# A gated scan and a mixture of experts on one core: one padded transpose per block, wider evictions, more row buffers

## The chip, the core and the metric

The kernel runs on one core of a Trainium2 chip. A core has five engines with queues of their own: PE (TensorE, matmuls), DVE (VectorE), ACT (ScalarE), POOL (GpSimd) and SP (SyncE, which here only issues transfers). Each takes its instructions strictly in the order of the program. The metric is device time of one execution, in microseconds; smaller is better.

## The reference

Two stages follow each other. The first is a gated linear recurrence over 5056 steps, for 4 sequences of 256 features; the second sends each of the 20,224 resulting rows to one of 8 experts, chosen by the largest of its 8 gate logits.

```python
a_t = exp(8 * sigmoid(r_gate) * log(clip(sigmoid(a_param), 1e-6, 1 - 1e-6)))
x_gated = sqrt(max(1 - a_t * a_t, 1e-6)) * sigmoid(i_gate) * x
for t in range(S):
    h = a_t[:, t] * h + x_gated[:, t]
    y[:, t] = h
...
e_idx = argmax(x @ w_gate, axis=1)               # x is now y, one row for each token
for e in range(8):
    rows = e_idx == e
    h = maximum(x[rows] @ w1[e], 0)              # 256 -> 1024
    out[rows] = gate_w[rows] * sigmoid(x[rows] @ w_output_gate)[e] * (h @ w2[e])
```

## The kernel before

**Work and order.** Each operation is described as a piece of `Work` with an engine, a cost, what it waits for and a rank; a planner (`in_order`) plays the list through and fixes the order of PE, DVE and ACT. The constants at the top of the file (ranks, costs, lags) set that order. SP and POOL issue in the order in which the pieces come out of it.

**Scan.** Tokens lie in 21 chunks: two of four tiles of 128 tokens, then of eight, the last of six. A block is up to four tiles, 512 tokens, with features on partitions (two halves of 128). For each block SP loads `rt`, `it` and `xt` (r_gate, i_gate, x; line 597, 512 KB each), from rings of 4, 3 and 2 buffers. ACT computes the gates (`gate_r` L603, `gate_i` L606, the decay L613, the square L617, the root L622), DVE the gated input (L609, L625) and the scan (L656).

**Routing.** From the third chunk on, DVE finds the peak of a chunk (L742), from it comes a scale (L760 to L764), and the states are split in two planes of 16 bit, a high part by ACT (`high`, L771) and a rest by DVE (`rest_of`, L774), written over the block's `rt` tile. PE takes the gate logits from the planes (L791), and DVE adds their three parts (L800 to L802), chooses the expert and counts positions. Beside this, SP turns the planes from features on partitions to tokens on partitions with DMA transposes (`flip`, L781), into row buffers `rows_all`, eight tiles deep. DVE writes a weight and a token number behind each row (`weights`, L891 and L892), and POOL scatters the rows by expert into a table `xs` in DRAM (L401), one indirect transfer for each tile.

**Experts.** A slot is 128 or 256 consecutive rows of one expert in `xs`. There are 104 slots at fixed places, worked off while the scan goes on, then 29 that are planned at run time (and a loop for more, which these inputs don't need). For a slot SP fetches the rows with a DMA transpose (`xt<-xs`, L1036). PE computes the hidden layer in eight blocks `f` of 128 (L1091, six matmuls each, into PSUM tiles `ph`, a ring of three); ACT evicts with a ReLU to the high part of `h` (L1106), DVE to the rest (L1109); PE multiplies with the second weights (L1148, into `po`); ACT scales (L1160, `ot`, two buffers) and POOL stores the 128 rows by an indirect transfer (L1163). One eviction covers two blocks `f`, so 256 columns for a slot of 128 rows and 512 for one of 256. The weights of the experts are loaded by ACT's queue and split in two planes in the first part of the run.

## Time and profile before

| | |
|---|---|
| time, median of 3 runs | 1096.76 us (1094.14 to 1097.5) |
| the profiled execution's own time | 1096.72 us |
| its span, first to last instruction | 1094.9 us |
| mean granted TensorE clock | 0.947 of full speed |
| PE, DVE, ACT, POOL busy | 954.1, 722.6, 639.2, 366.0 us |
| indirect transfers of POOL (L401, L1163) | 158 and 165 |
| DMA transposes on SP (L781, L1036) | 152 and 133 |

Busy is the time in which an engine ran something; matmuls are pipelined, so a busy PE need not be at its peak. A row of the profile names line, engine, operation and tiles as output<-input. SPq and POOLq are the queues of these engines, where transfers are issued and waits are held. In brackets behind a row stands the idle time of the engine just before it, and what ended it.

### The profile page before, as it was taken

To read this page: it belongs to the slowest core of one execution; us is meant where nothing else is said; L and a number is where in the kernel's file an instruction comes from. 1 tells how busy PE (TensorE), PEld (TensorE's weight loads), DVE (VectorE), ACT (ScalarE), POOL (GpSimd) and SP (SyncE) were. 2 spreads that over 40 slices of the span, in tenths; PEclk is the share of its full clock that TensorE was granted. 3 is DMA by queue.
4 is the path that set the end of the run, shared out by engine and by line. 5 is a ranking of instruction groups with operands and counts; after the bars stand their busy time and mean duration, and the time that the engine had idled before them with its cause. 6 is when DMAs were issued, how large, how long until landed. Compare 5 with 4: busy or idle time off the path is not lost. (4 is left out here: it accounts for less than half of the span.)

```text
span 1094.9 us, 30254 instructions
## 1 busy us (share of the span) xinstructions
PE 954.1 (87%) x11462; PEld 875.1 (80%) x11462; DVE 722.6 (66%) x1987; ACT 639.2 (58%) x1137; POOL 366.0 (33%) x341
## 2 busy tenths in 40 slices
PE   2628369998899899899999999999999999999993
PEld 1527368888889889888988887888888889999992
DVE  4898998878778769877987687778622222343330
ACT  5995977757757757776786667764222222333331
POOL 1112343353336236344633353435322122121111
PEclk9659679999999999999999999999999999999997
DMA  9969588886877967989887766755612213999970
GB/s 335 391 218 224 160 192 195 152 210 174 204 168 177 200 157 179 191 203 183 187 207 201 187 172 195 200 129 118 199 51 52 54 45 114 246 238 240 242 200 14
DMA packets 263764, 197.22 MB, mean 180 GB/s; under 512 B 203036, under 2 KB 214046, under 8 KB 263616
## 3 DMA queue, kind: packets, MB, share of 16 engines
q1 hardware_dynamic: 237536, 136.23, 53.7%
q0 software_dynamic: 15552, 42.23, 11.8%
q10 hardware_dynamic: 10528, 16.78, 4.4%
q8 instruction: 95, 1.56, 0.6%
q14 instruction: 53, 0.43, 0.2%
HBM read 79.09 MB, written 45.28 MB: 114 GB/s over the span
## 5 line engine op out<-in xcount | busy, mean ns | idle before, releaser
L1148 PE MATMUL po<-w2r,h 128*128 128x256 f16 (+1 forms) x3960 | 523.4, 275 | 1.2 <-ACT ot L1160 0.9
L1091 PE MATMUL ph<-xt,w1r 128*128 128x128 f16 (+1 forms) x4992 | 436.4, 239 | 56.4 <-DVE h L1109 43.0
L1091 PEld LDWEIGHTS <-w1r 128*128 128x128 f16 x4992 | 369.0, 100 | 84.7 <-issue 55.6
L1148 PEld LDWEIGHTS <-h 128*128 128x128 f16 x3960 | 372.6, 99 | 40.5 <-ACT h L1106 0.8
L1109 DVE SCALAR_TENSOR_TENSOR h<-ph,h 128x256 f16<-128x256 f32 (+1 forms) x532 | 236.4, 481 | 222.2 <-ACT h L1106 219.3
L1163 POOL DMA_INDIRECT out_dram<-ot,osc x165 | 185.9, 1127 | 490.1 <-ACT h L1106 264.4
L1106 ACT ACTIVATE h<-ph 128x256 f16<-128x256 f32 (+1 forms) x532 | 209.1, 431 | 185.5 <-PE po L1148 158.0
L401 POOL DMA_INDIRECT xs<-rows_all,posi x158 | 176.6, 1118 | 214.7 <-ACT h L1106 74.4
L1160 ACT ACTIVATE ot<-po,osc 128x256 f32<-128x256 f32 x165 | 74.3, 471 | 120.3 <-PE po L1148 66.2
L1091 PE MATMUL ph<-xt,ws 128*128 128x128 f16 x1392 | 98.4, 219 | 0.0
L656 DVE TENSOR_TENSOR_SCAN it<-rt,last,it 128x512 f32<-128x512 f32 (+4 forms) x78 | 96.0, 1240 | 0.4
L1091 PEld LDWEIGHTS <-ws 128*128 128x128 f16 x1392 | 88.4, 98 | 2.9
L609 DVE SCALAR_TENSOR_TENSOR xt<-it,xt 128x1024 f32<-128x1024 f32 (+1 forms) x40 | 48.2, 1207 | 42.6 <-ACT it L606 35.8
L606 ACT ACTIVATE it<-it 128x1024 f32<-128x1024 f32 (+1 forms) x40 | 41.8, 1044 | 57.7 <-DMA it<-in_i_gate_dram 57.6
L625 DVE SCALAR_TENSOR_TENSOR it<-it,xt 128x1024 f32<-128x1024 f32 (+1 forms) x40 | 48.2, 1205 | 21.9 <-ACT it L622 21.9
L613 ACT ACTIVATE rt<-rt,lam 128x512 f32<-128x512 f32 (+1 forms) x80 | 62.0, 803 | 0.9 <-issue 0.3
L774 DVE SCALAR_TENSOR_TENSOR rt<-it,scale,rt 128x1024 f16<-128x1024 f32 (+1 forms) x38 | 47.6, 1266 | 10.6 <-ACT rt L771 10.2
L617 ACT ACTIVATE it<-rt 128x1024 f32<-128x1024 f32 (+1 forms) x40 | 41.8, 1044 | 18.2 <-DVE xt L609 18.0
L603 ACT ACTIVATE rt<-rt 128x1024 f32<-128x1024 f32 (+1 forms) x40 | 41.9, 1046 | 13.2 <-DMA rt<-in_r_gate_dram 11.7
L742 DVE TENSOR_REDUCE peak<-it 128x1 f32<-128x1024 f32 (+1 forms) x38 | 45.4, 1196 | 0.0
L622 ACT ACTIVATE it<-it,quarter 128x1024 f32<-128x1024 f32 (+1 forms) x40 | 45.2, 1137 | 0.3
L771 ACT ACTIVATE rt<-it,scale 128x1024 f16<-128x1024 f32 (+1 forms) x38 | 42.3, 1133 | 2.2 <-DVE scale L764 2.1
(168 smaller groups left out, 564.8 us busy)
## 6 DMA issues: line engine op xcount, KB each, us to landing
ws<-w1r SPq DMA_DIRECT2D x58, 512.0 KB
rt<-in_r_gate_dram SPq DMA_DIRECT2D x39, 512.0 KB
it<-in_i_gate_dram SPq DMA_DIRECT2D x39, 512.0 KB
xt<-in_x_dram SPq DMA_DIRECT2D x39, 512.0 KB
w1r<-in_moe_w_dram ACTq DMA_DIRECT2D x7, 1024.0 KB
w2r<-in_moe_w_dram ACTq DMA_DIRECT2D x7, 1024.0 KB
out_dram<-ot,osc POOLq DMA_INDIRECT x165
xs<-rows_all,posi POOLq DMA_INDIRECT x158
```

What stands on the lines that cost most here:

```text
L401: op = nc.gpsimd.indirect_dma_start(out=xs[:, :], out_offset=bass.IndirectOffsetOnAxis(ap=pos, axis=0), in_=rows.bitcast(F32), in_offset=None,
L609: nc.vector.scalar_tensor_tensor(t("xt"), t("it"), 1.0, t("xt"), op0=ALU.add, op1=ALU.mult)
L613: nc.scalar.activation(r[:, h], r[:, h], AF.Exp, scale=lam[:, h:h + 1], bias=lam[:, h:h + 1])
L625: nc.vector.scalar_tensor_tensor(t("it"), t("it"), 0.5e-3, t("xt"), op0=ALU.max, op1=ALU.mult)
L656: nc.vector.tensor_tensor_scan(H[:, h, lo:hi], A[:, h, lo:hi], H[:, h, lo:hi], first, op0=ALU.mult, op1=ALU.add)
L774: nc.vector.scalar_tensor_tensor(halves(key, 1, m), tiles["it", key][:, :, 0:m], tiles["scale_of", c], halves(key, 0, m), op0=ALU.mult, op ...
L1091: nc.tensor.matmul(ph[:, i, 0:w], lhsT=ws[:, f // 2 % 2, a, c, i * P:(i + 1) * P], rhs=xt[:, b * ND + c, 0:w], start=k == 0, stop=k == 3 * ...
L1106: newest["relu"] = nc.scalar.activation(part(0, f0), tiles["ph", s, f0][:, :, 0:w], AF.Relu).ins
L1109: nc.vector.scalar_tensor_tensor(part(1, f0), tiles["ph", s, f0][:, :, 0:w], 0.0, part(0, f0), op0=ALU.max, op1=ALU.subtract)
L1148: nc.tensor.matmul(po[0:pw, j], lhsT=hh[:, a, f % 4, j * P:j * P + pw], rhs=second(b), start=f + j + a + b == 0, stop=f == NF - 1 and a == ...
L1160: nc.scalar.activation(ot[0:pw], tiles["po", s][0:pw, j], AF.Copy, scale=tiles["osc", s][0:pw, j, 0:1])
L1163: op = nc.gpsimd.indirect_dma_start(out=out[:, :], out_offset=bass.IndirectOffsetOnAxis(ap=tiles["osc", s][0:pw, j, 1:2].bitcast(I32), axi ...
```

## The change

- **Planes.** The two planes of a block lie tile by tile, 640 elements apart, of which 512 are data. `high` and `rest_of` write them in this form; `rest_of` becomes two instructions and clears the gaps between the tiles. One DMA transpose turns the whole block, 19 groups of 128 columns for four tiles, where before there were four transposes of four. The row buffers have the same pitch of 640, so the transposed padding covers the place of weight and token number, and `weights` waits for the transposes.
- **Logits.** Their three parts are added by one reduction.
- **Evictions.** A PSUM tile holds four blocks `f` of a slot of 128 rows, and one eviction covers them, 512 columns. For slots of 256 rows nothing changes.
- **Buffers.** Twelve row buffers in place of eight, three `xt` buffers in place of two; GpSimd's scratch for transfer descriptors is set to 4096 bytes; a small tile is kept in 16 bit, and one that nothing reads is left out.
- **A drain** of GpSimd's queue stands behind the store of the slot that is eight before the end.
- **Planner.** Costs, lanes of transfers in flight and all ranks are new; the decay is described in four pieces in place of one.

```diff
-XT = 2
-ROWS = 8
+XT = 3
+ROWS = 12
+PITCH = 640
+PLANE = 2 * PITCH - P // 2
-LAG = 0.0015
+LAG = 0.00132
...
+    RETIRE = n_slots - GROUP - 8
...
+        def plane(key, k, h, j):
+            at = j * PITCH + (k * ND + h) * P
+            return tiles["planes", key][:, at:at + P]
...
         def rest_of(key, m):
-            nc.vector.scalar_tensor_tensor(
-                halves(key, 1, m), tiles["it", key][:, :, 0:m], tiles["scale_of", c], halves(key, 0, m), op0=ALU.mult, op1=ALU.subtract
-            )
-
-        def flip(b, key, k, m):
+            if m > P:
+                a = plane(key, 2, 0, 0)
+                nc.vector.memset(bass.AP(a.tensor, a.offset, [a.ap[0], [PITCH, m // P - 1], [1, P]]), 0.0)
+            for h in range(ND):
+                nc.vector.scalar_tensor_tensor(
+                    halves(key, 1, m // P)[:, :, h], of_tiles(key, m)[:, :, h], tiles["scale_of", c], halves(key, 0, m // P)[:, :, h],
+                    op0=ALU.mult, op1=ALU.subtract,
+                )
+
+        def flip(b, key, m):
             nb = m // P
-            for h in range(ND):
-                queue("SP", nc.sync.dma_start_transpose(
-                    rows_all[:, row_at[b]:row_at[b] + nb, (k * ND + h) * P:(k * ND + h + 1) * P], halves(key, k, m)[:, h],
-                ))
+            to = rows_all[:, row_at[b]:row_at[b] + nb, :].rearrange("p j (k d) -> p (j k) d", d=P)
+            runs = nb * PITCH // P - 1
+            queue("SP", nc.sync.dma_start_transpose(to[:, 0:runs], tiles["planes", key][:, 0:runs * P]))
...
-            u = small.tile([P, 4, 2 * E], F32, name=f"lt_{c}_{b}", tag="lt", bufs=1)[:, 0:nb]
-            nc.vector.tensor_copy(u, t[:, :, 2])
-            nc.vector.tensor_tensor(u, u, t[:, :, 1], op=ALU.add)
-            nc.vector.tensor_tensor(st("lz", 2 * E)[:, b:b + nb], u, t[:, :, 0], op=ALU.add)
+            nc.vector.tensor_reduce(st("lz", 2 * E)[:, b:b + nb], t.rearrange("p j k e -> p j e k"), axis=AX.X, op=ALU.add)
...
-        wt = work("DVE", 0.68, weights, [zs], quick, uses=rused)
+        wt = work("DVE", 0.73, weights, [zs] + flips, quick, uses=rused)
...
-        for f0 in range(0, NF, 2):
+        g = 2 * SLOT // w if WIDER else 2
+        for f0 in range(0, NF, g):
             pu, pold = rings["ps_h"].new()
-            for i in range(2):
+            for i in range(g):
...
+                if s == RETIRE:
+                    queue("Pool", nc.gpsimd.drain(fusable=False), "out")
...
-    nc = _bacc.Bacc("TRN2", target_bir_lowering=False, num_devices=1)
+    nc = _bacc.Bacc("TRN2", target_bir_lowering=False, num_devices=1, dynamic_dma_scratch_size=4096)
```

The tables of ranks show little in themselves; what they do is seen in the order of the instructions. The first place is SP's queue at the tenth chunk: the transposes of its first block (`rt_0`) and second (`rt_4`), the i_gate loads (`it_4`, `it_0`) of the blocks after it, and the next slot's fetch (`xt<-xs`). Before:

```order
L781 DMA_TRANSPOSE rows_all<-rt_0_4325 128x4x128 x4
L597 DMA it_4_5859<-in_i_gate_dram 128x2x512
L597 DMA it_0_5874<-in_i_gate_dram 128x2x512
L597 DMA rt_0_5927<-in_r_gate_dram 128x2x512
L1028 TENSOR_LOAD firsti_5250
L1036 ISA
L1036 DMA_TRANSPOSE xt_40_5991<-xs 128x4x128
```

and now:

```order
L626 DMA it_4_5428<-in_i_gate_dram 128x2x512
L626 DMA it_0_5441<-in_i_gate_dram 128x2x512
L823 DMA_TRANSPOSE rows_all<-rt_0_4351 128x19x128
L823 DMA_TRANSPOSE rows_all<-rt_4_4472 128x19x128
L1065 TENSOR_LOAD firsti_3577
L1073 ISA
L1073 DMA_TRANSPOSE xt_39_5557<-xs 128x4x128
```

The loads have moved from behind the first block's four transposes to a place ahead of both blocks' transposes; in other chunks the first load stands ahead of the first block's transpose and the second between the two. The second block's transposes follow at once, where before they stood behind two more fetches.

The second place is DVE's queue in the same chunk, just ahead of `weights` (it ends with the write to `rows_all`). The names are `h` for an eviction, `osc` for a slot's scales, `it` for the scan. Before:

```order
L872 TENSOR_REDUCE sm_6014<-ex_5982 128x8
L873 TENSOR_REDUCE zs_6012<-df_5970 128x8
L609 SCALAR_TENSOR_TENSOR xt_4_5581<-it_4_5859,xt_4_5581 128x1024
L1109 SCALAR_TENSOR_TENSOR h_1_6017<-ph_4_5943,h_1_6017 128x2x128
L1109 SCALAR_TENSOR_TENSOR h_1_6017<-ph_6_5972,h_1_6017 128x2x128
L1121 TENSOR_SCALAR osc_6072<-mt_5628,tab 128x1
L1122 SCALAR_TENSOR_TENSOR osc_6072<-again_3700,mt_5628 128x1
L880 TENSOR_SCALAR zs_6012<-zs_6012 128x8
L881 SCALAR_TENSOR_TENSOR sm_6014<-sm_6014,zs_6012 128x8
L885 TENSOR_SCALAR sm_6014<-sm_6014,scale_5733 128x8
L891 RECIPROCAL rows_all<-sm_6014 128x8
```

and now:

```order
L1147 SCALAR_TENSOR_TENSOR h_0_5735<-ph_0_5661,h_0_5735 128x4x128
L685 SCALAR_TENSOR_TENSOR it_0_4780<-rt_0_4973,last_4_5220,it_0_4780 128x512
L688 COPY last_0_5779<-it_0_4780 128x2
L1147 SCALAR_TENSOR_TENSOR h_1_5776<-ph_4_5713,h_1_5776 128x4x128
L1159 TENSOR_SCALAR osc_5813<-mt_5377,tab 128x1
L1160 SCALAR_TENSOR_TENSOR osc_5813<-again_3580,mt_5377 128x1
L917 TENSOR_SCALAR zs_5604<-zs_5604 128x8
L918 SCALAR_TENSOR_TENSOR sm_5606<-sm_5606,zs_5604 128x8
L922 TENSOR_SCALAR sm_5606<-sm_5606,scale_5302 128x8
L928 RECIPROCAL rows_all<-sm_5606 128x8
```

`weights` has moved behind the counts of the chunk and a scan of the next; between the second block's split and the write to `rows_all` there now stand seven evictions of 512 columns, two scans and three instructions of 1024 columns, and some thirty small ones.

## Rows read from the trace of the kernel before

**Rows 1.** The page: busy time, share of the span, instructions.

```profile
PE 954.1 (87%) x11462; PEld 875.1 (80%) x11462; DVE 722.6 (66%) x1987; ACT 639.2 (58%) x1137; POOL 366.0 (33%) x341
```

**Rows 2.** Busy time by stretch: length, engines, PEclk (granted clock), DMA share, GB/s.

```profile
0.00:219.00 219.00, 133.24 (x1607) 121.56 (x1608) 185.31 (x489) 171.24 (x258) 60.35 (x64) 0.82 0.85 234
219.00:739.00 520.00, 484.54 (x6081) 444.95 (x6080) 411.25 (x1088) 361.33 (x622) 224.81 (x197) 0.98 0.77 185
739.00:1067.00 328.00, 326.87 (x3672) 300.31 (x3671) 123.39 (x403) 103.35 (x249) 77.93 (x78) 1.00 0.56 150
1067.00:1095.00 28.00, 9.45 (x109) 8.31 (x106) 2.64 (x10) 3.32 (x9) 2.95 (x3) 0.71 0.04 14
```

**Rows 3.** Waits from 219 to 739 us: total, times, longest.

```profile
PE ph L1091 <- DVE h L1109: 28.5, 17, 3.7
...
PE pk L862 <- DVE oh L856: 5.9, 3, 2.7
```

**Rows 4.** Timeline of one stall: start, duration, operation, count, idle before.

```profile
349.94 5.53 SPq L781 DMA_TRANSPOSE rows_all<-rt  x4
349.94 1.28 DVE L774 SCALAR_TENSOR_TENSOR rt<-it,scale,rt 128x1024 f16<-128x1024 f32 x1 [0.37 <-ACT rt L771]
...
355.52 1.12 SPq L597 DMA_DIRECT2D it<-in_i_gate_dram  x2
...
362.09 1.06 ACT L606 ACTIVATE it<-it 128x1024 f32<-128x1024 f32 x1 [3.69 <-DMA it<-in_i_gate_dram]
...
363.05 0.64 ACT L1106 ACTIVATE h<-ph 128x256 f16<-128x256 f32 x2
...
364.79 1.51 PE L1091 MATMUL ph<-xt,w1r 128*128 128x128 f16 x17 [3.65 <-DVE h L1109]
```

**Rows 5.** Waits from 219 to 739 us, of ACT and DVE for transfers.

```profile
ACT it L606 <- DMA it<-in_i_gate_dram: 49.3, 22, 5.1
...
DVE rows_all L891 <- DMA xs<-rows_all,posi: 3.1, 2, 2.7
```

**Rows 6.** The end: timeline of PE and POOL; drains (min/median/max ns).

```profile
1071.50 4.95 PE L1148 MATMUL po<-w2r,h 128*128 x42
...
1077.29 0.98 POOL L1163 DMA_INDIRECT out_dram<-ot,osc  x1 [1.88 <-ACTq L1243]
...
L1271 POOLq DRAIN  x3: 40/103/9216, 1084.9 to 1094.7; - x3
```

**Rows 7.** Transposes of SP (L781 all, L1036 from 780 to 905), min/median/max ns.

```profile
L781 SPq DMA_TRANSPOSE rows_all<-rt x152: 1167/1258/2377, 85.4 to 767.5; - x152
...
L1036 SPq DMA_TRANSPOSE xt<-xs x13: 1217/1247/2135, 780.1 to 903.3; - x13
```

**Rows 8.** Groups by shape; last row: L1109 alone from 0 to 219 us.

```profile
L1109 DVE SCALAR_TENSOR_TENSOR h<-ph,h 128x256 f16<-128x256 f32 x404 | 153.6, 417 | 118.6 <-ACT h L1106 116.1 <-ACT ot L1160 1.4
L1106 ACT ACTIVATE h<-ph 128x256 f16<-128x256 f32 x404 | 137.9, 379 | 101.2 <-PE po L1148 76.2 <-PE ph L1091 18.7 <-DVE lt L800 2.5
...
L1109 DVE SCALAR_TENSOR_TENSOR h<-ph,h 128x512 f16<-128x512 f32 x128 | 82.8, 683 | 103.6 <-ACT h L1106 103.3
L1106 ACT ACTIVATE h<-ph 128x512 f16<-128x512 f32 x128 | 71.1, 594 | 84.3 <-PE po L1148 81.8 <-PE ph L1091 2.3
L774 DVE SCALAR_TENSOR_TENSOR rt<-it,scale,rt 128x1024 f16<-128x1024 f32 x37 | 47.0, 1280 | 10.6 <-ACT rt L771 10.2
...
L802 DVE TENSOR_TENSOR lz<-lt,lg 128x64 f32<-128x64 f32 x37 | 8.2, 221 | 1.3
...
0.00:219.00 219.00, 22.88 (x62) 0.82 0.85 234
```

**Rows 9.** Timeline: the fills of the start; transposes and first scatter of a chunk.

```profile
16.85 6.00 SPq L388 DMA_DIRECT2D xs<-zrow  x2
...
403.10 5.56 SPq L781 DMA_TRANSPOSE rows_all<-rt  x4
...
412.41 1.98 POOL L401 DMA_INDIRECT xs<-rows_all,posi  x1 [0.30 <-DVE osc L1122]
```

More of the change, by code (lines that the diff above doesn't have):

```diff
@@ L83, with __init__ @@
 class Work:
-    __slots__ = ("engine", "time", "emit", "after", "rank", "table", "dma", "slack", "left", "next", "follow", "ready", "start", "end", "index", "late", "ring")
-    def __init__(self, engine, time, emit, after, rank, table=None, dma=0.0, slack=0.0):
+    __slots__ = ("engine", "time", "emit", "after", "rank", "table", "dma", "slack", "left", "next", "follow", "ready", "start", "end", "index", "late", "ring", "lanes", "lead")
+    def __init__(self, engine, time, emit, after, rank, table=None, dma=0.0, slack=0.0, lanes=1, lead=DMA_START):
+        self.lanes, self.lead = lanes if dma and engine in ("SP", "ACT") else 0, lead
         self.slack, self.ring = slack, RINGS.get(engine, 0)
@@ L151, in in_order @@
             heapq.heappush(later[w.engine], (0.0, w.index, w))
-    table, queued, shared, order = None, [0.0, 0.0, 0.0], 0.0, []
+    table, queued, shared, order = None, [0.0, 0.0, 0.0], FIRST_DMA, []
     window, active, warm = 0, 0.0, False
+    lane, issued = [0.0] * LANES, 0
     while True:
@@ L187, in in_order @@
             cost = at - t
+        begun = t
+        if w.lanes:
+            at = t
+            for k in range(w.lanes):
+                at = max(at, lane[(issued + k) % LANES]) + cost / w.lanes
+            begun, cost = at - cost, at - t
         w.start = t
@@ L191, in in_order @@
         if w.dma:
-            queued, shared = drained(queued, max(0.0, t + DMA_START - shared)), max(shared, t + DMA_START)
+            queued, shared = drained(queued, max(0.0, begun + w.lead - shared)), max(shared, begun + w.lead)
             queued[w.ring] += w.dma
             w.end = shared + lasts(queued, w.ring) + DMA_DONE
+            for k in range(w.lanes):
+                lane[issued % LANES] = w.end
+                issued += 1
         order.append((t, len(order), w))
@@ L264, in queue, with work @@
         return ins
-    def work(engine, time, emit, after=(), rank=0.0, table=None, dma=0.0, uses=(), slack=0.0):
-        w = Work(engine, time, emit, after, rank, table, dma, slack)
+    def work(engine, time, emit, after=(), rank=0.0, table=None, dma=0.0, uses=(), slack=0.0, lanes=1, lead=DMA_START):
+        w = Work(engine, time, emit, after, rank, table, dma, slack, lanes, lead)
         w.late = late[-1] if late else 0
@@ L465, in load @@
                     )
-            loads.append(work(WEIGHTS_BY, {"SP": DMA_ISSUE, "ACT": 0.1}[WEIGHTS_BY], load, [old] + loaded.get(u - DEPTH, []), UNIT_LOAD[u], dma=2.6 / g, uses=[use]))
+            loads.append(work(WEIGHTS_BY, {"SP": DMA_ISSUE, "ACT": 0.4}[WEIGHTS_BY], load, [old] + loaded.get(u - DEPTH, []), UNIT_LOAD[u], dma=2.6 / g, uses=[use]))
             parts.append(use)
@@ L484, in square @@
         def square():
-            dg = small.tile([P, P], F32, name=f"dg_{u}", tag="dg", bufs=1)
+            dg = small.tile([P, P], BF16, name=f"dg_{u}", tag="dg", bufs=1)
             sq = tiles["sq", u] = small.tile([P, 1], F32, name=f"sq_{u}", tag="sq")
@@ L928, in chunk @@
         quick = rank + QUICK
-        ch = work("DVE", 0.35, choose, lows, quick)
+        ch = work("DVE", 0.41, choose, lows, quick)
         ex = work("ACT", 0.25, chances, [ch], quick, "E")
@@ L1063, in fetch_weights @@
             queue("SP", nc.sync.dma_start(ws.rearrange("p q h c f -> p (q h c f)"), w1r[:, bass.ds(tiles["eo", s] + k * size, size)]))
-        fw = work("SP", 2.0, fetch, [ready, xold, mold] + routed[c] + fills[:1 + (c >= wide)], rank, dma=0.3 + 1.7 * scale, uses=[xu, mu, vuse])
+        fw = work("SP", 2.2 + 0.5 * scale, fetch, [ready, xold, mold] + routed[c] + fills[:1 + (c >= wide)], rank, dma=0.3 + 1.7 * scale, uses=[xu, mu, vuse], lanes=2, lead=2.2)
         every = [v for u in range(2 * E) for v in split[u]] if s == len(static) else []
@@ L1111, in slot @@
             hu, hold = hus[f0 // 4]
-            m = work("ACT", 0.11 + 0.425 * scale, relu, [m, hold], rank, uses=[pu, hu])
-            evac.append(work("DVE", 0.08 + 0.53 * scale, low, [m], rank, uses=[pu, hu]))
+            m = work("ACT", 0.11 + 0.2125 * g * scale, relu, [m, hold], rank, uses=[pu, hu])
+            evac += [work("DVE", 0.08 + 0.265 * g * scale, low, [m], rank, uses=[pu, hu])] * (g // 2)
         ou, oold = rings["osc"].new()
```

118 lines of the change are left out of this document (67 added, 51 removed).

## The prediction

> **What bounds the kernel now.** I began with the page's busy times: TensorE is busy 87% of the span, DVE 66%, ACT 58% [rows 1]. An average over unlike stages says little, so the next view is the busy time by stretch [rows 2]. It shows four stages. From 0 to 219 us TensorE works 133 of 219 us, and DVE (185 us) and ACT (171 us) are nearly full: the scan of the first chunks, the splitting of the weights and the first routing run ahead of any expert work. From 219 to 739 us TensorE works 484.5 of 520 us, so 35.5 us are lost. From 739 to 1067 us it works 326.9 of 328 us: nothing but less matmul work would help there, and the change leaves the matmuls as they are. The last 28 us hold 9.5 us of matmuls and a tail. So what can be won lies in three places: the start, the 35.5 us of the middle, and the tail.
>
> The middle was read with the list of waits. Of TensorE's idle time there 28.5 us are waits of the first layer's matmuls for DVE's eviction (17 of them), 5.9 us are rank matmuls that wait for the one-hot table [rows 3]; together 34.4 of the 35.5 us. The timeline of one stall shows what stands behind "waits for DVE" [rows 4]. SP is taken for 5.53 us, from 349.94 us on, by the four transposes of one block, and only then, at 355.52, issues the two i_gate loads. ACT, whose queue is in order, reaches gate_i, waits 3.69 us for that load and starts it at 362.09. The two evictions of `ph` queued behind it start only at 363.05, DVE's evictions behind them, and TensorE, whose PSUM buffers are all full, has waited 3.65 us. So the late step is a load, late because SP was transposing. It repeats in each chunk: in this stretch ACT waits 22 times for i_gate loads, 49.3 us in all [rows 5].
>
> The tail: the last matmul ends at 1076.45, the last store ends at 1078.27, and the span ends at 1094.9 us. One instruction fills half of the rest, a DRAIN in GpSimd's queue of 9216 ns; the shortest of the three there takes 40 ns [rows 6].
>
> **The change, part by part.** The sum is made against the profiled execution's own time, 1096.72 us, which is 1.8 us more than its span and equals the median of the runs shown (1096.76) within 0.1 us.
>
> *Transposes and loads on SP.* Before, a block cost four issues at a median of 1.258 us [rows 7]. Now it costs one, of 19 blocks of 128 columns in place of four times four. What that one takes, the trace doesn't show. From below it is one issue, 1.25 us; from above 19/4 of the old one, 5.97 us. The nearest rows are the fetches of `xt`: between 780 and 905 us they turn eight blocks each (slots of 256 rows), and their median is 1247 ns [rows 7]. So issue time did not grow from four blocks to eight, and I take 2.5 us, near the lower end. More important is the order: the rows printed above show one or both i_gate loads ahead of the transposes instead of behind four of them. Its buffer is that of a tile which DVE's split (L774) frees at 351.22 us in [rows 4], so the first load can leave 4.3 us earlier than at 355.52. That is more than the 3.69 us that ACT waited: the wait should go, and TensorE's 3.65 us with it. The transposes move 19/16 of their bytes; the DMA engines are busy 77% of the middle [rows 2] and nothing there waits for transposed rows, so I cost that at nothing. Without that cover it would be a sixth more of the old four issues, 0.9 us a block.
>
> *Evictions.* The 404 narrow evictions become 202 of 512 columns. DVE takes 417 ns for 256 columns and 683 for 512 (busy, with overlap, 153.6/404 = 0.380 and 82.8/128 = 0.647 us each), ACT 379 and 594 (0.341 and 0.555) [rows 8]. DVE saves 153.6 - 202 x 0.647 = 22.9 us over the run, ACT 137.9 - 202 x 0.555 = 25.8. These lie beside matmuls almost everywhere and aren't added to the sum. What they buy is cover: a PSUM buffer now holds four blocks of the hidden layer, so the three hold 12 where they held 6, and a late eviction stops TensorE later.
>
> *The split of a block* on DVE becomes two instructions of 512 columns and a memset: 2 x 0.683 + 0.22 (an estimate: the memset as one small instruction of DVE, such as L802) against 1.280 us, 0.31 us more for each of 37. The logit sum becomes one reduction in place of three instructions of 0.221; it costs between one such and all three, and as it reads all three parts I take 0.35, an estimate near the middle, and save 0.31 each [rows 8]. They cancel.
>
> *A new wait:* `weights` on DVE now waits for the transposes to land, since their padding covers the place it writes. Behind it in DVE's queue stand evictions. The order puts far more ahead of it: in the chunk shown, between the second block's split and this write, 7 wide evictions (4.8 us), three of 1024 columns (3.7 us), two scans (2.6 us) and some 30 small ones (about 5 us), 16 us together. Two issues of 2.5 us, and then the landing: in the old trace the first scatter starts at 412.41 us, 3.75 us after the four issues that began at 403.10 ended [rows 9], so landing takes at most that. That is 8.8 us, or 15.7 with the upper bound of both issues. No stall, though the last margin is thin. The scatters come later by as much as this write does, and the slots' order moves with them.
>
> *Twelve row buffers and a third x buffer* take away the 3.1 us that DVE waited in the middle for old scatters [rows 5]; that lies beside matmuls. *Smaller scratch*: no GpSimd instruction shows a wait for descriptor room. From below it costs nothing; from above each of the 323 indirect transfers would wait out the one ahead, priced under the rivals. I take nothing.
>
> *Middle.* The 34.4 us hang on late loads; I take 23 off, leaving about 12 of the 35.5 for the longer split, the later scatters and reordered queues. Bounds: 10 (only one of two loads in time) to 33.
>
> *Start.* 62 narrow evictions fall in it: DVE saves 22.88 - 31 x 0.647 = 2.8 us, ACT by its means 62 x 0.341 - 31 x 0.555 = 3.9 [rows 8]. The second of two fills leaves the start, where both took 6.00 us of SP [rows 9], so 3.0 there. DVE and ACT are what this stage waits for; much of their work lies side by side, so I count the larger saving alone, 4 us. Bounds: 9.7, if the three add along one chain, and -6, if the new ranks put as much in its way as the two fills took.
>
> *Tail.* The change puts a drain behind the store eight slots before the end, where GpSimd is busy 78 of 328 us [rows 2]. If the 9.2 us is bookkeeping that grows with the transfers since the last drain (40 ns right after another points there), 7 stores out of 323 leave about 0.6 us: 8.6 saved. If it is fixed, 0.
>
> Sum: 1096.7 - 23 - 4 - 8.6 = **1061 us**.
>
> **The rivals.**
> *A: the merged issue is no cheaper than its parts.* Two blocks take 2 x 5.97 = 11.9 us of SP. The first load still comes early, the second and the fetches behind late; the middle gives 10, the start nothing. 1096.7 - 10 - 8.6 = 1078. For it: SP's issues of four blocks never fell under 1167 ns. Against: eight blocks cost what four do [rows 7].
> The Trainium skill, page "DMA: Bandwidth & Descriptors", section "Why a DMA increments its semaphore by 16 and not by 1", lists for chips before the newer generation 262,144 sequencer cycles for an SBUF to SBUF transpose of 8,192 tiles, a cost that grows with tiles. By that rule the time would be rival A's. The trace disagrees for fetches from DRAM, 1247 ns for eight blocks; for SBUF sources no row here shows it.
>
> *B: slower, by the new wait on DVE.* If transposes land later than 16 us after the split, DVE stands still in each of 19 chunks, evictions behind it. It cancels the gain at 36/19 = 1.9 us a chunk; with 4 us it is 1061 + 76 = 1137. Against: 15.7 us even by the upper bound.
>
> *C: slower, by the scratch.* If each indirect transfer waits for the one ahead (1.1 us of issue plus 2 us), 16 in a chunk take 50 us, where a chunk has some 37: 19 x 13 = 250 us more. Against: nothing in the trace speaks for so little room.
>
> *D: little comes of it.* The drain stays 9.2 us, the new order of the start costs 6 us and the middle gives 10: 1093.
>
> **How the numbers follow.** The forecast 0.64 (1045 to 1077), A 0.16, D 0.08, B 0.08, C 0.04. The time is the forecast's, 1061. The range reaches from 1043 (middle 33, start 9.7, drain 8.6 would be 1045, and 2 for the uncounted) to 1090, which takes in A and the better part of D and leaves out B, C and the rest of D. About 0.3% (3 us) is what a measurement of this kernel can tell from no change: faster 0.84, same 0.04 (half of D), slower 0.12.
>
> **What would show it.** Right: ACT's wait for i_gate under 15 us in the middle, TensorE idle there near 12 us, SP's transpose issue under 3 us, `weights` not waiting for a DMA, the final DRAIN under 1 us, TensorE still full after the scan has ended. Wrong: 6 us issues (A), DVE idle in front of `weights` (B), GpSimd transfers of 3 us (C), a DRAIN of 9 us (D).

## The result and the profile after

The changed kernel takes 1044.56 us (median of 4 runs, 1041.86 to 1045.63) against 1097.13 of the kernel before in the same session: a ratio of 0.9501, 95% interval 0.9435 to 0.9567. The profiled execution spans 1040.2 us, 54.7 less than before.

The stores of GpSimd tell where it was won, since there are 165 of them in both kernels and they keep pace with the matmuls. The table gives, from the timelines of GpSimd in the two profiles, the start of the 17th, 65th, 73rd, 105th and last store and the end of the span, as differences:

| us | to 17th | to 65th | to 73rd | to 105th | to last | to the end |
|---|---|---|---|---|---|---|
| before | 236.0 | 291.0 | 61.1 | 183.2 | 306.0 | 17.6 |
| after | 223.2 | 276.5 | 51.8 | 177.6 | 303.1 | 8.0 |
| saved | 12.8 | 14.5 | 9.3 | 5.6 | 2.9 | 9.6 |

So the start gave 12.8 us, the middle with what follows it 32.3, the tail 9.6. Up to each of these stores the two kernels have done nearly the same matmuls, so the stretch from the 17th to the 105th (29.4 us shorter) can be split by TensorE's busy time, the first number behind the length:

```profile
236.02:771.32 535.30, 502.15 (x6198) 460.14 (x6196) 425.44 (x1149) 362.61 (x626) 232.33 (x204) 0.98 0.76 180
```

```profile
223.23:729.10 505.87, 495.62 (x6213) 458.00 (x6211) 427.65 (x1098) 355.65 (x522) 237.69 (x210) 0.99 0.93 208
```

Idle time went from 33.2 to 10.3 us, so 22.9 us of the 29.4 are idle time, and 6.5 us are matmuls that ran faster. The page's busy times of the changed kernel, and its view by stretch for the first two stages (columns as in [rows 2]):

```profile
PE 945.2 (91%) x11462; PEld 871.8 (84%) x11462; DVE 708.7 (68%) x1798; ACT 623.7 (60%) x931; POOL 365.5 (35%) x341
```

```profile
0.00:219.00 219.00, 143.18 (x1751) 131.41 (x1752) 188.56 (x472) 172.16 (x232) 65.75 (x68) 0.81 0.85 241
219.00:700.00 481.00, 472.04 (x6016) 437.08 (x6014) 415.65 (x1041) 351.09 (x512) 229.98 (x203) 0.99 0.95 210
```

In these stretches, cut where the scan ends, TensorE now idles 9.0 of 481 us, where it idled 35.5 of 520. Its waits there, and those of ACT and DVE for transfers, which answer to [rows 3] and [rows 5] (total, times, longest):

```profile
PE ph L1129 <- DMA xt<-xs: 5.4, 3, 2.7
...
PE ph L1129 <- DVE h L1147: 0.9, 1, 0.9
...
ACT rt L632 <- DMA rt<-in_r_gate_dram: 15.7, 8, 3.6
...
ACT it L635 <- DMA it<-in_i_gate_dram: 3.4, 5, 1.4
...
DVE rows_all L928 <- DMA out_dram<-ot,osc: 2.2, 1, 2.2
```

The wait for r_gate loads has grown (5.4 us before) while that for i_gate loads has all but gone.

Idle time is not the whole gain. Two slices of 20 us, the first of before, the second of after, show a stall's second price: the granted clock (the number behind the five busy times) falls to 0.91 on average. That is some 3.6 us at 1.2 GHz in place of 2.4 (0.09 x 20 / 0.5), so 1.8 us of work. The microsecond shown third, in the kernel before, lies behind the stall of [rows 4] that ends at 364.79: TensorE is busy all through it, at half the clock.

```profile
360.00:380.00 20.00, 16.35 (x198) 14.93 (x196) 14.58 (x40) 16.24 (x28) 5.11 (x5) 0.91 0.94 181
```

```profile
380.00:400.00 20.00, 16.83 (x221) 15.29 (x220) 13.57 (x36) 13.13 (x21) 8.41 (x8) 0.91 1.18 256
```

```profile
366.00:367.00 1.00, 1.00 (x11) 0.99 (x10) 0.90 (x7) 0.98 (x4) 0.51 (x1) 0.50 0.67 132
```

Between 220 and 740 us there were six such slices before (at 0.91 or 0.92), each with a stall or behind one, and there are two after: about 7 us that no list of waits shows, which agrees with the 6.5 us above. Not every stall has this price: before, one of 2.41 us that ends at 403.90 leaves its slice at 1.00.

SP's rows of the changed kernel: the loads do stand ahead of the transposes, but an issue of 19 groups takes over 4 us in both places shown. The median over all 38, of which 37 have 19 groups, is 4.70 us (columns as in [rows 7]).

```profile
390.09 0.39 SPq L626 DMA_DIRECT2D it<-in_i_gate_dram  x1
390.53 4.32 SPq L823 DMA_TRANSPOSE rows_all<-rt  x1
...
398.19 0.39 SPq L626 DMA_DIRECT2D it<-in_i_gate_dram  x1
398.76 4.18 SPq L823 DMA_TRANSPOSE rows_all<-rt  x1
```

```profile
L823 SPq DMA_TRANSPOSE rows_all<-rt x38: 1411/4702/6312, 92.0 to 687.5; - x38
```

The tail, as in [rows 6]: the final DRAIN is 1.61 us in place of 9.22, and the early one takes 4.44 us, in which two scatters of GpSimd also run (at 724.00 and 725.27). In the trace it does not stand near the end: it comes behind the last scatter and ahead of the 105th store, so 61 of the 165 stores follow it.

```profile
L1314 POOLq DRAIN  x3: 46/103/1608, 1037.7 to 1039.9; - x3
```

```profile
L1209 POOLq DRAIN  x1: 4437/4437/4437, 723.8 to 723.8; - x1
```

### The profile page after: what moved, and what is told of

Its sections match the earlier page's. It is cut to its first block, busy times and chain, and to the rows that moved or that the text cites. A ratio compares the mean times of both kernels' runs of the same rounds, so it can differ in the third digit from the quotient of the medians.

```text
span 1040.2 us, 29569 instructions
## 1 busy us (share of the span) xinstructions
PE 945.2 (91%) x11462; PEld 871.8 (84%) x11462; DVE 708.7 (68%) x1798; ACT 623.7 (60%) x931; POOL 365.5 (35%) x341
## 3 DMA queue, kind: packets, MB, share of 16 engines
q0 software_dynamic: 15552, 42.23, 12.8%
## 4 chain that ended last, share of the span: by engine, by line
PE 64%; issue 9%; DVE 7%; DMA 6%; ACT 3%; POOL 2%; SPq 1%; POOLq 0%; ACTq 0%; DVEq 0%
PE ph L1129 32%; PE po L1186 30%; DMA xt<-xs 3%; POOL out_dram L1201 2%; DMA xs<-rows_all,posi 1%; DMA rt<-in_r_gate_dram 1%; SPq L823 1%; PE lg L831 1%; DVE h L1147 1%; DVE it L685 1%; DVE rt L814 1%; ACT rt L807 1%; DMA it<-in_i_gate_dram 0%; ACT w1r L548 0%; DVE w1r L558 0%
## 5 line engine op out<-in xcount | busy, mean ns | idle before, releaser
L1186 PE MATMUL po<-w2r,h 128*128 128x256 f16 (+1 forms) x3960 | 557.5, 274 | 7.8 <-ACT h L1144 5.6
L1129 PE MATMUL ph<-xt,w1r 128*128 128x128 f16 (+1 forms) x4992 | 463.5, 238 | 20.8 <-DMA xt<-xs 11.2
L1129 PEld LDWEIGHTS <-w1r 128*128 128x128 f16 x4992 | 377.5, 99 | 47.9 <-issue 8.7
L1186 PEld LDWEIGHTS <-h 128*128 128x128 f16 x3960 | 362.5, 98 | 43.4 <-ACT h L1144 5.7
L1147 DVE SCALAR_TENSOR_TENSOR h<-ph,h 128x512 f16<-128x512 f32 x330 | 223.0, 684 | 239.8 <-ACT h L1144 238.7
L1144 ACT ACTIVATE h<-ph 128x512 f16<-128x512 f32 x330 | 192.5, 592 | 236.6 <-PE ph L1129 149.4
L1129 PE MATMUL ph<-xt,ws 128*128 128x128 f16 x1392 | 106.1, 219 | 0.0
L1129 PEld LDWEIGHTS <-ws 128*128 128x128 f16 x1392 | 92.4, 98 | 3.9
L814 DVE SCALAR_TENSOR_TENSOR rt<-it,scale,rt 128x512 f16<-128x512 f32 (+1 forms) x76 | 50.2, 701 | 12.4 <-ACT rt L807 12.3
L654 DVE SCALAR_TENSOR_TENSOR it<-it,xt 128x1024 f32<-128x1024 f32 (+1 forms) x40 | 48.2, 1205 | 14.2 <-ACT it L651 14.1
L635 ACT ACTIVATE it<-it 128x1024 f32<-128x1024 f32 (+1 forms) x40 | 41.7, 1042 | 10.1 <-DMA it<-in_i_gate_dram 5.7
L646 ACT ACTIVATE it<-rt 128x1024 f32<-128x1024 f32 (+1 forms) x40 | 41.7, 1043 | 7.9 <-DVE xt L638 6.3
```

What stands on the lines that cost most here:

```text
L654: nc.vector.scalar_tensor_tensor(t("it"), t("it"), 0.5e-3, t("xt"), op0=ALU.max, op1=ALU.mult)
L814: nc.vector.scalar_tensor_tensor(halves(key, 1, m // P)[:, :, h], of_tiles(key, m)[:, :, h], tiles["scale_of", c], halves(key, 0, m // P)[ ...
L1129: nc.tensor.matmul(ph[:, i, 0:w], lhsT=ws[:, f // 2 % 2, a, c, f % 2 * P:(f % 2 + 1) * P], rhs=xt[:, b * ND + c, 0:w], start=k == 0, stop= ...
L1144: newest["relu"] = nc.scalar.activation(part(0, f0), tiles["ph", s, f0][:, :, 0:w], AF.Relu).ins
L1147: nc.vector.scalar_tensor_tensor(part(1, f0), tiles["ph", s, f0][:, :, 0:w], 0.0, part(0, f0), op0=ALU.max, op1=ALU.subtract)
L1186: nc.tensor.matmul(po[0:pw, j], lhsT=hh[:, a, f % 4, j * P:j * P + pw], rhs=second(b), start=f + j + a + b == 0, stop=f == NF - 1 and a == ...
```

## The experiments

Ratios are to the kernel before on the same chip; the changed kernel's is 0.9501, and 0.1% is 1.1 us. The runs come from five chips, on which the kernel before took 1099 to 1108 us, so times in us from different runs compare to about 1%. The interval of 0.9501 reaches 0.7% to each side; a_halves and a_no_drain below, which come out as fast, have 0.3%. Two theories are set against each other. **Late loads** (the prediction's): TensorE stalls because SP transposes before it issues the i_gate loads, and moving the loads is the gain. **Cover**: ACT and DVE evict late at some place in every chunk whatever SP does, and what pays is how far TensorE can run ahead (PSUM's depth) and what the planner puts in front of the evictions.

### The load order alone: b_loads_first, b_loads_room, b_room, a_loads_late

In the kernel before, the order that the planner gives is kept on PE, DVE, ACT and GpSimd, and each i_gate load is moved ahead of the transposes in front of it on SP:

```diff
-    return [w for _, _, w in sorted(order, key=lambda v: v[:2])]
+    done = [w for _, _, w in sorted(order, key=lambda v: v[:2])]
+    for w in [w for w in done if w.kind == "it"]:
+        deps = set()
+        for item in w.after:
+            deps |= {id(d) for k in item for d in k} if isinstance(item, tuple) else {id(item)}
+        i = j = done.index(w)
+        at = i
+        while j and id(done[j - 1]) not in deps and (done[j - 1].engine != "SP" or done[j - 1].kind == "flip"):
+            j -= 1
+            at = j if done[j].kind == "flip" else at
+        done.insert(at, done.pop(i))
+    return done
```

> The kernel before with one difference: in SP's queue each i_gate load is issued ahead of the transposes that stood in front of it; the order on the four other engines is the same row for row. Theory of the order (loads late because SP transposes): ACT's wait for i_gate in the middle falls from 49.3 us to under 15, TensorE's wait for DVE's evictions there from 28.5 to under 8, the time to about 1070 us (1060 to 1077). Theory of the cover (narrow evictions and shallow PSUM are what lets a stall reach TensorE): ACT's wait falls as well, but TensorE's wait stays above 20 us and the time above 1087. A third outcome, the transposes now late and the scatters behind them, would show as waits of TensorE for xt.

It is slower, 1.0146 (1.0119 to 1.0173), which is on the side of cover. Its waits from 219 to 739 us, of TensorE, ACT and SP:

```profile
PE ph L1106 <- DVE h L1124: 45.3, 26, 6.8
...
ACT rt L615 <- DMA rt<-in_r_gate_dram: 26.2, 7, 7.7
...
ACT it L618 <- DMA it<-in_i_gate_dram: 19.8, 9, 4.5
...
SPq L609 <- DMA rows_all<-rt: 19.8, 14, 6.3
```

The i_gate wait fell from 49.3 to 19.8 us, the way that late loads says though not under 15, and TensorE's rose from 28.5 to 45.3. The last row tells why: the planes lie in `rt` buffers, and a transpose that is issued later also lands later; the next r_gate load waits for it on SP (19.8 us, before 4.2), and ACT waits for that load instead (26.2, before 5.4). The wait moved from one load to the other.

b_loads_room takes that second wait away by more buffers, under the same order; b_room has the buffers without the order:

```diff
-                bufs = rings[tags[k]].n
+                bufs = {"rt": 5, "it": 4}.get(tags[k], rings[tags[k]].n)
...
+    nc = _bacc.Bacc("TRN2", target_bir_lowering=False, num_devices=1, dynamic_dma_scratch_size=4096)
```

> The kernel before with the i_gate loads ahead of the transposes as in b_loads_first, and with five rt and four it buffers in place of four and three, so that neither the i_gate nor the r_gate load waits for transposes (scratch of 4096 bytes makes the room; the order on all engines is that of b_loads_first). Against b_scratch: by the theory of late loads ACT's waits for both loads in the middle fall under 20 us together, TensorE idles under 12 us there and the time is 15 to 25 us under b_scratch. By the rival (the order of routing and evictions on DVE and ACT, and PSUM's depth) the loads come in time, TensorE's waits for DVE's evictions stay above 20 us, and the time is within 6 us of b_scratch.

> The kernel before with scratch of 4096 bytes, five rt and four it buffers, and SP's order unchanged (transposes ahead of the i_gate loads): b_loads_room without its order. If the order of the loads is what b_loads_room gained (ratio 0.9777 against 0.9923 of b_scratch), this stays at 0.989 to 0.995 with ACT's i_gate waits over 35 us; if the buffers alone gained it, 0.974 to 0.982.

The ratios are 0.9777 (0.9742 to 0.9813) and 0.9926 (0.9900 to 0.9953); the scratch alone has 0.9923 (below). So the buffers alone give nothing, and with them the load order gives 1.5%, some 16 us. That is within the range that late loads named, but TensorE's wait for evictions hardly moved: 24.8 us, where under 12 was expected and b_scratch has 26.2. What went is the wait of the rank matmuls for the one-hot table, 7.5 us in b_scratch and none here. The theory has part of the gain and not its stated way. b_room adds to this: there the buffers alone bring ACT's i_gate wait down to 30.5 us (47.2 in b_scratch; over 35 was expected), and the time doesn't move.

```profile
PE ph L1106 <- DVE h L1124: 24.8, 20, 5.5
...
ACT rt L615 <- DMA rt<-in_r_gate_dram: 20.3, 7, 6.4
...
ACT it L618 <- DMA it<-in_i_gate_dram: 11.9, 7, 4.0
```

The row of b_scratch that is gone:

```profile
PE pk L862 <- DVE oh L856: 7.5, 3, 3.6
```

In a_loads_late the same function, with the two kinds exchanged, puts the changed kernel's transposes ahead of the loads.

> The changed kernel with each block's transpose issued ahead of the i_gate loads that stood in front of it, all other engines in the same order. Theory of the order: ACT's wait for i_gate comes back (over 35 us in the middle), TensorE idles 30 us or more there in place of 9, and the time goes up by 20 to 35 us. Theory of the cover: ACT waits again, but twelve blocks of the hidden layer in PSUM carry TensorE across most of it; TensorE idles under 18 us and the time goes up by less than 10.

1.0562 (1.0535 to 1.0590), more than three times the loss that late loads forecast. ACT, TensorE and SP from 219 to 739 us:

```profile
ACT it L647 <- DMA it<-in_i_gate_dram: 93.2, 15, 9.5
...
PE pk L913 <- DVE oh L907: 42.7, 7, 8.0
...
SPq L836 <- ACT h L1158: 25.3, 16, 3.0
```

The new order needs its loads early. TensorE now stops mostly at the rank matmuls, which wait for DVE's one-hot table, and less at the evictions (14.1 us). The loss is more than SP's issue time, though: the last row shows SP held in front of the moved transposes by what the profile gives as evictions of ACT (1.2 us in the changed kernel), with the loads behind it.

### Width and depth: a_narrow, a_halves, a_ring2, b_deep

```diff
-WIDER = True
+WIDER = False
```

> The changed kernel with evictions of two blocks (256 columns) for slots of 128 rows, so PSUM holds six blocks in place of twelve; the planner orders the matmuls anew for it. Theory of the order: +2 to +6 us, from the start alone. Theory of the cover: TensorE's waits for DVE's evictions in the middle go from 1 us to over 20, the time up by 20 to 35 us.

0.9849 (0.9817 to 0.9881): 3.5% are lost, some 38 us, a little more than cover forecast. From 219 to 739 us:

```profile
PE ph L1129 <- DVE h L1147: 26.4, 29, 4.5
```

The wait of [rows 3] is back with nearly its old sum, while ACT's waits stay at 8.6 us for i_gate and 15.1 for r_gate in the same stretch. Stalls of this kind need no late load. By the stores, 29.5 us are lost up to the 17th (252.7 us) and only 10.8 more up to the 105th. So most of what the width is worth lies in the start; and from the 17th to the 105th store the narrow kernel, at 516.7 us, still has 18.6 of the 29.4 us that the change gained there.

```diff
-                newest["relu"] = nc.scalar.activation(part(0, f0), tiles["ph", s, f0][:, :, 0:w], AF.Relu).ins
+                for i in range(0, g, 2):
+                    newest["relu"] = nc.scalar.activation(part(0, f0, i), tiles["ph", s, f0][:, i:i + 2, 0:w], AF.Relu).ins
...
```

and the same for DVE's eviction, without a change of plan:

> The changed kernel with the same order and the same PSUM tiles, but each eviction of 512 columns of a slot of 128 rows issued as two of 256: DVE busy +23 us, ACT +26, cover nearly unchanged. If the width pays through DVE's and ACT's time, this costs what a_narrow costs, and the start gets 4 us longer; if it pays through the depth of PSUM, under 5 us in all and TensorE's waits in the middle stay under 15 us.

0.9509 (0.9481 to 0.9536), no difference at all, and the 17th store comes at 222.5 us, as in the changed kernel. The time that ACT and DVE save by wide evictions is worth nothing here, in the start neither. What the width buys is elsewhere: in the blocks that PSUM holds and in the order that this allows.

```diff
-    ps_h = ctx.enter_context(tc.tile_pool(name="ps_h", bufs=3, space=bass.MemoryType.PSUM))
+    ps_h = ctx.enter_context(tc.tile_pool(name="ps_h", bufs=2, space=bass.MemoryType.PSUM))
...
```

and the same in the planner's table of rings:

> The changed kernel with two PSUM tiles of four blocks in place of three (eight blocks of the hidden layer in PSUM; before had six, the changed kernel twelve), planned anew with the same ranks and wide evictions. If depth is what the width buys, TensorE's waits for DVE's evictions come back to 15 us or more in the middle and the ratio lies between 0.965 and 0.99; if the number of evictions or the plan counts, it stays under 0.958.

1.0090 (1.0070 to 1.0109): with eight blocks in PSUM in place of twelve, 5.9% are lost, more than forecast, and TensorE waits as never before:

```profile
PE ph L1129 <- DVE h L1147: 41.2, 26, 5.2
```

From the 17th to the 105th store it takes 552.1 us (505.9 in the changed kernel). The new ranks with this PSUM are worse than the old kernel, which had six blocks. But the count of blocks is not the whole of it: a_narrow holds six under the same ranks, in three tiles, and loses less than eight in two. Each is planned anew, and no run separates the number of tiles from the number of blocks. b_deep gives the kernel before the depth without a new plan:

```diff
+                    if i == 0 and (w > P or f0 % 4 == 0):
+                        tiles["bank", s] = ps_h.tile([P, 2 * SLOT // w, w], F32, name=f"ph_{s}_{f0}", tag="ps_h")
                     if i == 0:
-                        tiles["ph", s, f0] = ps_h.tile([P, 2, SLOT], F32, name=f"ph_{s}_{f0}", tag="ps_h")
+                        k = f0 % 4 if w == P else 0
+                        tiles["ph", s, f0] = tiles["bank", s][:, k:k + 2]
```

> The kernel before, every engine's instructions in the same order and the same size, but for slots of 128 rows two PSUM tiles of 256 columns lie in one bank, so that three banks hold twelve blocks of the hidden layer in place of six. If the depth alone carries TensorE across late evictions, its waits for DVE's evictions in the middle fall from 28.5 us to under 12 and the time to about 1070 to 1080 us. If the depth pays only together with an order of matmuls that runs ahead, the waits move to the second layer (po waits for h) or stay, and the time stays within 6 us of before.

1.0187 (1.0165 to 1.0209). It does not tell what it was meant to. Matmuls now also wait for ACT's evictions, 23 times, which they did nowhere in this stretch before. Two halves now share a tile, so that a matmul into one half waits for the eviction of the other is the likely reason; no run shows it apart:

```profile
PE ph L1094 <- ACT h L1109: 22.7, 23, 2.4
PE ph L1094 <- DVE h L1112: 9.6, 15, 1.0
```

The plain wait for DVE did fall (28.5 to 9.6), so depth works on it; but what it would give under the old order stays open. Two cleaner kernels were not run: the changed order itself with two tiles, and wide evictions alone in the kernel before.

### Ranks: a_oldranks, a_oldnarrow, a_tail_old, a_old_tail, a_start_old, a_steady_old

All but a_tail_old are the changed kernel with many numbers of the table put back, a_tail_old with one. The planner's costs and lanes stay new, so the order that comes out of the old ranks is not that of the kernel before. a_oldranks puts back every rank with LAG, QUICK, ROOT and SLACK; a_oldnarrow has narrow evictions besides.

> All code of the change with the ranks of before: of two by two (ranks old or new, evictions narrow or wide) the corner old and wide; the corners new and wide (1044.6) and new and narrow (1084.0) are measured. i_gate loads stand behind transposes in most chunks. If the new ranks' order of loads is what pays, over 1080 us with ACT's waits for i_gate over 40 us in the middle; if wide evictions pay under any order, 1050 to 1065.

> The fourth corner: all code of the change with the ranks of before and narrow evictions. If merged transposes, more buffers and the drain are worth little without ranks and width, it gives the time of before less the tail, 1085 to 1092 us; if wide evictions have the same price under both sets of ranks, it is some 40 us above a_oldranks.

| ratio to before | narrow | wide |
|---|---|---|
| old ranks | 1.0176 (1.0149 to 1.0202) | 1.0056 (1.0035 to 1.0078) |
| new ranks | 0.9849 (0.9817 to 0.9881) | 0.9501 (0.9435 to 0.9567) |

Ranks are worth 3.3% with narrow evictions and 5.5% with wide ones, width 1.2% under the old ranks and 3.5% under the new: together more than one by one. a_oldranks is over 1080 us, as the order of loads would have it, but with i_gate waits of 14.9 us where over 40 were expected, so late i_gate loads are not what it loses by; a_oldnarrow missed both its cases. All code of the change under the old ranks loses to the kernel before, although the tail is 9 us shorter. Some 23 of the 61 us between a_oldranks and the changed kernel are a single wait of TensorE for DVE's product (`dp`), from which a chunk's scale comes:

```profile
PE lg L784 <- DVE dp L780: 23.0, 1, 23.0
```

```diff
-TAIL = -779.074
+TAIL = -7.492
```

> The changed kernel with one number back: the rank that puts the routing of a chunk (peak, split in planes, logit sums) ahead of the evictions, -779 to -7.5. By the theory that this priority pays (the splits come early, so buffers and loads come early, and PSUM's depth covers the evictions that are pushed back) i_gate waits come back and the time rises by 20 to 60 us, in the start and the middle. If the ranks of loads and transposes alone pay, it rises by under 8 us.

0.9626 (0.9591 to 0.9660): routing ahead of the evictions is worth 1.25%, 14 us, between the two forecasts, and i_gate waits grow only to 11.2 us (3.4 in the changed kernel). TensorE waits for row fetches (12.7 us, longest 9.3; 5.4 in the changed kernel). The same number put alone into the old ranks:

> The converse: all code of the change with the ranks of before (a_oldranks, ratio 1.0056 to before) and the routing's rank alone new. If that rank carries the gain, most of the 5.5% between a_oldranks and the changed kernel comes back (ratio under 0.975); if it needs the others, the ratio stays over 0.99.

0.9991 (0.9964 to 1.0019), 0.65% better than a_oldranks. This one rank does not carry the gain.

a_start_old puts back what only the start has (UNIT_, CHUNK_, STEP_, LOW_ and GRAM_RANK, UNIT_ and CHUNK_LOAD, TABLES, FILL), a_steady_old the others (SLOT_, LOAD_, ROWS_ and LOGIT_RANK, TAIL, LAG, QUICK, ROOT, EARLY, SLACK).

> The changed kernel with the old ranks of everything that only the start has (weights, loads and steps of the first chunks, fills). If the start's 12.8 us come from these ranks, the time up to the 17th store goes from 223 back to 236 or more and the rest stays within 5 us of the changed kernel; if they come from wide evictions and early routing, it stays under 228.

> The changed kernel with the old ranks of everything that repeats in each chunk (slots, loads, transposes, routing, logits, roots). If the middle's gain comes from these ranks, the stretch from the 17th to the 105th store goes from 506 us to 530 or more, with i_gate waits over 30 us; if width carries it, under 515.

0.9999 (0.9979 to 1.0019) and 1.0253 (1.0231 to 1.0275). The first loses 66.6 us up to the 17th store (289.8 us) and nothing after it (501.8 us from the 17th to the 105th): the start's ranks decide the start. The second takes 575.6 us from the 17th to the 105th store (505.9 in the changed kernel), but with i_gate waits of 21.0 us; its largest wait is again the one of a_oldranks, here 44.9 us in two. In its own stretch, half a set of ranks does worse than the whole old set: with that (a_oldranks) the 17th store comes at 251.1 us, and 540.1 us pass from it to the 105th. So 66.6 us is the price of a mixture, not what the start's new ranks are worth.

### The tail: b_scratch, a_no_drain

```diff
-    nc = _bacc.Bacc("TRN2", target_bir_lowering=False, num_devices=1)
+    nc = _bacc.Bacc("TRN2", target_bir_lowering=False, num_devices=1, dynamic_dma_scratch_size=4096)
```

> The kernel before with GpSimd's scratch at 4096 bytes, nothing else. If the scratch is what shortened the tail, the final DRAIN falls from 9.2 us to under 2, the end comes 7 to 9 us after the last store in place of 17.6, and the time falls by 8 to 10 us. If the early drain is needed too, the DRAIN stays over 4 us. If a small scratch makes transfers wait (rival C), the indirect transfers of GpSimd take longer than 1.12 us on average and the time rises.

0.9923 (0.9895 to 0.9951), 8.4 us. From the last store to the end it takes 7.8 us (17.6 before); indirect transfers keep their length (1126 and 1137 ns on average, before 1127 and 1118).

```profile
L1271 POOLq DRAIN  x3: 40/103/804, 1081.7 to 1084.0; - x3
```

```diff
-                if s == RETIRE:
-                    queue("Pool", nc.gpsimd.drain(fusable=False), "out")
```

> The changed kernel without the drain behind the store of the slot eight before the end, nothing else. If the final DRAIN grows with the transfers since the last one, it returns from 1.61 us to about 6 (1.61 and the 4.44 that the early one takes) and the time goes up by 4 to 5 us; if the smaller scratch is what shortened it, it stays under 2.5 us and the time is the same; if neither, 9.2 us and 8 us more.

0.9500 (0.9471 to 0.9528), no difference, and the final DRAIN is shorter without the early one:

```profile
L1312 POOLq DRAIN  x3: 40/103/804, 1044.9 to 1046.2; - x3
```

The scratch alone shortened the tail; the drain does nothing for the time.

### Merging and row buffers: a_four, a_rows8

```diff
-            queue("SP", nc.sync.dma_start_transpose(to[:, 0:runs], tiles["planes", key][:, 0:runs * P]))
+            for k in range(0, runs, 5):
+                n = min(5, runs - k)
+                queue("SP", nc.sync.dma_start_transpose(to[:, k:k + n], tiles["planes", key][:, k * P:(k + n) * P]))
```

> The changed kernel with each block's 19 groups turned by four transposes of five groups (the last of four) in place of one, all engines in the same order. If an issue costs by its groups (before: 1.258 us for four, 0.31 each; the changed kernel: 4.70 us for 19, 0.25 each), four take 4 x 1.25 to 4 x 1.6 = 5.0 to 6.3 us, and the ratio is 0.950 to 0.958. If merging is what freed SP, SP's transposes take over 7 us a block, i_gate waits come back and the ratio is over 0.965.

0.9659 (0.9619 to 0.9699): the ratio is that of the second case, but the issue is that of the first, five groups in 1.274 us:

```profile
L825 SPq DMA_TRANSPOSE rows_all<-rt x150: 1035/1274/2683, 91.3 to 723.3; - x150
```

Four are 5.10 us by the median, one merged issue 4.70. The merging is worth 1.6% (17 us), and 0.4 us of SP a block does not explain that; i_gate waits don't come back (3.2 us). From 219 to 739 us TensorE idles 24.5 us (10.3 in the changed kernel), and 11.1 of them stand under "issue", where the profile shows nothing that was waited for; a_rows8, from the same chip, has 7.8 us of that kind and the changed kernel none, so a part may belong to the chip. The cause stays open.

```diff
-ROWS = 12
+ROWS = 8
```

> The changed kernel with eight row buffers in place of twelve, planned anew. If row buffers only take away waits beside matmuls, the ratio stays at 0.948 to 0.958; if transposes behind a full ring hold SP and with it the loads, SP's waits for scatters in front of transposes go from 16.5 us to over 60 and the ratio is over 0.97.

0.9837 (0.9802 to 0.9872), the second case. From 0 to 739 us, SP's waits:

```profile
SPq L626 <- DVE it L654: 73.1, 18, 16.7
...
SPq L823 <- DMA xs<-rows_all,posi: 62.3, 17, 6.0
SPq L626 <- DVE rt L814: 46.3, 23, 11.1
```

A transpose that waits for a row buffer holds SP, and every load and fetch is queued behind it; in the changed kernel the three rows are 43.5, 16.5 and 25.8 us. In the kernel before, with eight buffers too, the middle one was 9.7 us: it is the new order that needs the twelve.

## Why the prediction was wrong, point by point

The forecast said faster, 1061 us. The measured ratio gives 1042 on the time before (0.9501 x 1096.76), just under the range's lower end of 1043; the interval, 1035 to 1049, reaches across it. In spans, 35.6 us were forecast and 54.7 came: start 4 against 12.8, middle 23 against 32.3, tail 8.6 against 9.6. **The steps that failed are the sizes of the start and of the middle**, and behind the middle's size a mechanism that was only part of the cause.

- **Middle, 23 us.** Its upper bound was 33, and it came near it. The 32.3 us are 22.9 of idle time and 6.5 of faster matmuls between the 17th and the 105th store, and 2.9 behind it that no run places. So the idle time came out as forecast, in part by luck, as the next point shows. What the sum lacked is a term for the clock, which fell to its lower level at six places before and at two after: 6.5 to 7 us. This was readable in the slices of the trace before.
- **"The wait should go, and TensorE's 3.65 us with it."** It went (49.3 to 3.4 us), but not for that reason alone. Moved by itself, the load makes the kernel slower, since the r_gate load then waits for the transposes; with buffers for both it gives 16 us. a_narrow shows that TensorE's waits are there again without late loads. The step "they buy cover" had named the right thing and gave it no number: without the depth and the order made for it, the stretch from the 17th to the 105th store is 10.8 us longer in a_narrow and 46.2 in a_ring2. How the 29.4 us of this stretch split between loads, depth and order stays open, since each part needs the others.
- **Start, 4 us.** The terms were the eviction time saved (2.8 and 3.9 us) and a fill. a_halves puts that eviction time back and loses nothing, so the term had no ground. What makes the start is the order: the 17th store comes 66.6 us later with the start's old ranks, 27.8 with all the old ranks, 29.5 with narrow evictions and the order planned for them. Which place of the order it is, and what the fill that left the start is worth, no run shows. A list of what each engine saves doesn't show that, and -6 to 9.7 as bounds were too tight.
- **Transposes, 2.5 us.** The measured 4.70 us is near rival A's 5.97. The nearest rows taken (fetches from DRAM, 1247 ns for eight groups) were of another kind of source. The rule of the Trainium skill, page "DMA: Bandwidth & Descriptors", section "Why a DMA increments its semaphore by 16 and not by 1", that a transpose from SBUF costs by its tiles, fits in direction only: 19 groups cost 3.7 times what four cost, and not 4.75 times, and five (1.274 us, a_four) cost no more than four. Rival A's time, 1078, still failed: with issues near its size the i_gate wait went all the same.
- **Row buffers, nothing.** DVE's 3.1 us were the wrong wait to look at. It is SP that waits for row buffers, with the loads behind it: 3.4%.
- **Tail, 8.6 us.** Right in size by luck, wrong in cause (and the last DRAIN is 1.61 us, not under 1). The drain was credited and the scratch costed at nothing; b_scratch and a_no_drain show the reverse. The working was off too: not 7 but 61 stores come after the drain, and 7 of 323 would have left 0.2 us, not 0.6.
- **Right:** the split of a block (two of 708 ns and a memset of 218, forecast 683 and 220), the logit sum (352 ns, forecast 350), DVE's `weights` not waiting for the transposes (rival B; one wait of 2.2 us in the whole run, put down to a store), indirect transfers no longer (rival C), ACT's i_gate wait under 15 us (3.4) and TensorE idle near 12 us in the middle (9.0), and TensorE full after the scan.

What stays open: how much depth alone gives under the old order, what in the order makes the start, and why four transposes in place of one cost 17 us. The losses from taking single parts back (row buffers 3.4%, width 3.5%, merging 1.6%, routing's rank 1.25%) add up to more than the whole gain; they hold one another up, so none of them is "the" share of a part. None of the kernels run beats the changed one; without the drain it is as fast.

## What to carry to other kernels

When a wait is to be removed by moving one issue ahead of another on an in-order queue, look up what the one moved back releases: here it was the buffer of the very next load. Wide evictions and deep PSUM pay by how far the matmuls may be ordered ahead of the evictions, not by the engine time that they save, so they and the order have to be judged together. And look behind each stall of TensorE for a stretch at the lower clock, which no list of waits contains.

## What the runs showed of the hardware

The last DRAIN of GpSimd's queue goes with the size of its descriptor scratch: 9216 ns with the default, 804 ns with 4096 bytes and the same 323 transfers; with a drain in between the two took 4437 ns (two scatters run inside it) and 1608 ns, so draining early shortened nothing. The time that a transpose from SBUF takes to issue is not fixed: for the same 19 groups the median is 4.70 us in the changed kernel and 3.36 us in a_rows8, where SP waits longer in front of them; so part of it looks like waiting for transfers already in flight, which no run here separates.
